# A new hand-written order of steps for a cross-attention kernel with a snake-activated feed-forward network

## The chip, the cores and the metric

The kernel runs on one core of one Trainium2 chip. Five engines work side by side: TensorE (PE in the profile, with its weight loads shown apart as PEld), VectorE (DVE), ScalarE (ACT), GpSimd (POOL) and SyncE (SP). Each engine takes its instructions strictly in the order in which the program gives them to it. The time is device microseconds for one launch, the median of several runs.

## The reference, cut to what matters

```python
B, H, S, Ns, D = (8, 8, 512, 32, 64)          # x: B,H,S,D    state: B,H,Ns,D
n_tokens, d_model, d_ff = (4608, 512, 2048)

def _attn_ref(x, state):
    scale = 1.0 / np.sqrt(D)
    a = softmax(scale * np.matmul(x, state.transpose(0, 1, 3, 2)))    # over the 32 states
    xread = np.matmul(a, state)
    a2 = softmax(scale * np.matmul(state, x.transpose(0, 1, 3, 2)))   # over the 512 positions
    sread = np.matmul(a2, x)
    return np.concatenate([xread, sread], axis=2)

def _moe_ref(x, w_in, w_out, alpha):
    h = x @ w_in
    s = np.sin(alpha * h)
    g = h + s * s / (alpha + 1e-09)
    return g @ w_out
```

(`softmax` stands here for the reference's four lines of maximum, exp, sum and division.) The result of the first function, as 8 batches of 512 + 32 tokens with 512 features each, is the input of the second. All inputs and the output are float32; the kernel computes in bfloat16 with float32 sums.

## The kernel before

**Tiles.** The 4352 tokens are cut into nine tiles: tile t = 0 to 7 holds the 512 positions of batch t, tile 8 the 8 x 32 state tokens of all batches. A tile is carried through 16 slices f of 128 hidden features. For tiles 0 to 7 the kernel does not multiply x-reads by `w_in`. It first forms M = state x `w_in` for the batch (steps `m`, `me`), and then h = M x softmax weights, two matmuls of 512 columns for each f. Tile 8 takes four matmuls of 256 columns with `w_in`.

**Steps.** The class `Steps` has one short method for each kind of step, and the string `ORDER` lists some 1,380 steps, each with its arguments, in the order in which they are emitted. That one list fixes the order of every engine's instructions, of every DMA queue, and of the eight PSUM banks (the bank number stands at the end of a PE step that opens a new result). The steps that matter here:

- `h.t.f.bank` (line 537; 543 for tile 8; `hg`, line 552, is one half of it): h of tile t, slice f, on PE. `si.t.f` (560): the sine on ACT. `sq.t.f.E` (201 on POOL or DVE, 569 on ACT): its square on engine E, where A is ACT, V is DVE and G is POOL. `gt.t.f` (576): g = s2 * (1/alpha) + h on DVE, which reads h from PSUM a last time and so sets its bank free.
- `o.t.st.f0.f1` (587): output rows st = 0 to 3 of the tile, slices f0 to f1, one PE matmul of 512 columns for each f; its weights are g. `oc.t.st.E` (595) copies the finished bank, `os` (602, 605) sends it to HBM from SP's queue. `oh`, `och`, `osh` are the same for 384 and 128 columns of one block of tile 7.
- For batch b: `lx` loads x (POOL's queue), `pk` (348) sorts it, `td` (389) transposes it by a DMA from SP's queue, `sc` (399) makes the scores on PE, `ex` (406) the exp on ACT, `rs`, `rr` (410, 416) sum and reciprocal on DVE, `nm` (201) the softmax weights on POOL, `ad` (440) their transpose by a DMA from SP's queue, after which `h.b` may start. Batch 1 transposes x on PE (`xt`, 376, copied by `xc`), batch 0 does both on PE (`xtq`, `at`). `w` (450), `cs` (461), `rc`, `xs` are the second softmax.
- `m.b.s.banks` (488) and `me.b.s.g.E` (496): slice s of M in two halves g, and their copies. `st_t`, `st_c` (340): the transposed states of batches 2 to 7; `s01_t`, `s01_k` (316) those of batches 0 and 1.
- `lq` loads x of batch 0 from SP's queue; `l_st`, `li.s`, `lo.s` load the states and the four slices of `w_in` and `w_out` from POOL's queue. `consts`, `zero` clear constant tiles on DVE, `exp_table` and `sin_table` (226) make ACT load a function table early, and `warm_up.n.cols.bank` (303) issues n matmuls on the cleared tile `warm`, whose result nobody reads.

**Buffers.** The two tiles that `si` and `sq` write come out of one ring of 10, the g tiles out of a ring of 38, the output tiles out of a ring of 6. The next of each waits until the oldest has been read.

```python
    for step in ORDER:
        name, *args = step.split(".")
        getattr(steps, name)(*(int(a) if a.isdigit() else a for a in args))
```

Of the kernel before, what the change touches and what calls it, by code (L numbers as in the profile page):

```python
# [21 lines left out]
touch_x l_s01 zero.1 touch lq.0.S ident_ consts warm_up.2.128.0 warm_up.2.128.1 warm_up.2.128.2  # L22
l_alpha lq.1.S zero.0 warm_up.6.512.3 exp_table lq.2.S identf.V lq.3.S s01_c.G l_st li.0 xq.0.A
s01_t.4 li.1 xtq.0.5 xq.1.A s01_k.1.V s01_k.0.A li.2 xtq.1.6 xc.0.0.0.V xq.2.A xc.0.0.1.V lo.0
al_t.7 xq.3.A xtq.2.0 al_c inva sc.0.0.1 lo.1 xc.0.1.0.A xtq.3.2 warm_up.2.128.3 ex.0.0
warm_up.2.128.4 lx.1.0.1 warm_up.2.128.5 xc.0.1.1.V warm_up.2.128.6 warm_up.2.128.7 rs.0.0 sc.0.1.0
li.3 st_t.0.3 ex.0.1 rr.0.0 st_t.1.4 lo.2 st_c.0.0.V st_c.0.1.A warm_up.2.128.5 warm_up.2.128.6
warm_up.2.128.1 st_c.1.0.A rs.0.1 warm_up.2.128.2 warm_up.2.128.7 nm.0.0.0.4.G warm_up.2.128.0
warm_up.2.128.5 st_c.1.1.A warm_up.2.128.3 warm_up.2.128.6 warm_up.2.128.1 rr.0.1 warm_up.2.128.2
sin_table warm_up.2.128.7 warm_up.2.128.0 nm.0.1.0.4.G at.0.0.5 warm_up.2.128.3 ac.0.0.V m.0.0.6.4  # L30
m.1.0.1.2 lo.3 at.0.1.7 me.0.0.0.V me.0.0.1.A warm_up.2.128.0 warm_up.2.128.3 me.1.0.1.A ac.0.1.V
hg.0.2.0.5 me.1.0.0.V hg.0.1.0.4 hg.0.2.1 hg.0.1.1 hg.0.0.0.0 lx.2.0.1 si.0.2 hg.0.0.1 m.1.1.6.3
si.0.1 m.0.1.7.2 hg.0.3.0.1 me.0.1.1.A sq.0.2.V hg.0.3.1 sq.0.1.G me.1.1.0.V me.1.1.1.A
# [12 lines left out]
si.0.12 o.0.0.10.11 o.0.3.9.11 sq.0.13.G ad.1 hg.0.15.0.2 sq.0.12.A o.0.1.10.12 hg.0.15.1 gt.0.12
o.0.2.8.10 si.0.15 o.0.2.10.11 gt.0.13 o.0.0.11.12 hg.0.14.0.4 sq.0.15.A hg.0.14.1 o.0.3.11.13
si.0.14 gt.0.15 o.0.0.12.13 o.0.1.12.13 o.0.3.13.14 sq.0.14.A pk.2.0.V o.0.1.13.14 pk.2.1.V h.1.2.5
gt.0.14 h.1.4.6 td.2 si.1.2 lx.3.0.1 h.1.0.2 si.1.4 o.0.0.13.15 sq.1.2.V h.1.1.4 si.1.0 gt.1.2
sq.1.4.G o.0.3.14.16 si.1.1 o.0.2.11.13 sq.1.0.A oc.0.3.V h.1.6.5 sq.1.1.G gt.1.4 o.0.2.13.14 os.0.3  # L50
h.1.3.0 si.1.6 gt.1.0 o.0.1.14.16 si.1.3 sq.1.6.G h.1.13.6 gt.1.1 oc.0.1.A o.0.2.14.15 o.0.0.15.16
si.1.13 h.1.15.2 sq.1.3.G gt.1.6 os.0.1 o.0.2.15.16 oc.0.0.A h.1.5.4 sq.1.13.G oc.0.2.V si.1.15
h.1.7.3 os.0.0 gt.1.3 o.1.1.0.1.5 si.1.5 os.0.2 h.1.8.1 sq.1.15.G gt.1.13 o.1.1.1.2 si.1.7
o.1.2.0.2.7 sq.1.5.A o.1.1.2.3 sq.1.7.G h.1.12.0 gt.1.15 si.1.8 h.1.9.6 gt.1.5 o.1.2.2.3 si.1.12
sq.1.8.G o.1.2.3.5 gt.1.7 si.1.9 o.1.1.3.4 h.1.10.2 sq.1.12.A pk.3.1.V h.1.11.4 sq.1.9.G gt.1.8
o.1.2.5.6 si.1.10 o.1.2.6.7 gt.1.12 h.1.14.3 si.1.11 sq.1.10.G o.1.2.7.8 gt.1.9 sc.2.1.1 si.1.14
o.1.1.4.7 sq.1.11.A pk.3.0.V sq.1.14.G o.1.1.7.8 gt.1.10 td.3 o.1.2.8.9 sc.2.0.0 o.1.1.8.9 gt.1.11
# [606 lines left out]
```

## Time and profile before

| what | value |
|---|---|
| median of 8 runs (lowest to highest) | 221.3 us (220.83 to 222.78) |
| the profiled execution: its own time / its span | 220.93 us / 219.0 us |
| PE busy, matmuls | 210.2 us (96%), 1593 recorded |
| ACT, DVE, POOL busy | 173.3 us (79%), 162.0 us (74%), 107.0 us (49%) |
| `o` matmuls (line 587) | 133.9 us busy, 542 recorded |
| `h` matmuls (line 537) | 60.0 us busy, 219 recorded |
| warm-up matmuls (line 303) | 7.4 us busy, 66 recorded |
| DMA transposes, issue to landing (median) | x 4.3 us (6 of them), softmax weights 3.2 us (7) |

The span runs from the first to the last instruction of the program, and the time of a run has about 2 us around it. A matmul's record is longer than the distance to the next one, since matmuls overlap; so the distance from start to start is what a matmul costs PE when it is kept fed. Some matmul records are missing (1593 of 1619), while every weight load is there; so the steps were found in the trace by their weight loads. Idle time is shown in brackets with what ended it.

### The profile page before, as it was taken

Reading aid. Unit: us, or ns where it says so; the run is one execution under the profiler, and the core shown is the slowest. Engines: PE = TensorE matmul, PEld = TensorE weight load, DVE = VectorE, ACT = ScalarE, POOL = GpSimd, SP = SyncE. Lnnn points to the kernel's source line nnn. Section 1 sums busy time; section 2 is a strip of 40 time slices with the busy share of each in tenths; the row PEclk is TensorE's granted clock in tenths of the full one; section 3 lists DMA queues with packets and bytes.
Section 4 is the critical chain, followed back from the end, with each engine's and each line's share of the span. In section 5 each row is a group of like instructions: output and inputs, shape, how many; then the busy total and the mean of one; then the engine's idle time right before and its main releaser. Section 6 shows DMA issues by size and latency. Waiting matters only on the chain.

```text
span 219.0 us, 4304 instructions
## 1 busy us (share of the span) xinstructions
PE 210.2 (96%) x1593; PEld 104.6 (48%) x1619; DVE 162.0 (74%) x286; ACT 173.3 (79%) x297; POOL 107.0 (49%) x115
## 2 busy tenths in 40 slices
PE   6889999999999999999999999999999999999994
PEld 2744544444444534444454444454445555665452
DVE  2769896999768889989888788888667987661201
ACT  4799878997899979898996999798848896785111
POOL 5968533895296657753943387273501082121000
PEclk9999999999999999999999999999999999999999
DMA  6999999945487529167145327480220211012042
GB/s 200 193 199 201 205 203 133 207 124 96 99 166 123 99 95 139 58 144 95 49 82 133 107 70 96 136 108 0 48 100 3 96 48 48 0 51 96 1 143 97
DMA packets 38052, 23.48 MB, mean 107 GB/s; under 512 B 20992, under 2 KB 33680, under 8 KB 38032
## 3 DMA queue, kind: packets, MB, share of 16 engines
q1 hardware_dynamic: 26128, 15.08, 27.2%
q0 software_dynamic: 11648, 8.13, 26.2%
q8 instruction: 12, 0.20, 0.4%
q14 instruction: 8, 0.07, 0.1%
q10 hardware_dynamic: 256, 0.01, 0.1%
HBM read 17.44 MB, written 8.91 MB: 120 GB/s over the span
## 4 chain that ended last, share of the span: by engine, by line
PE 88%; ACT 4%; DVE 4%; issue 2%; POOL 2%
PE o_ps L587 52%; PE h_ps L537 20%; PE m_ps L488 4%; PE h_ps L543 3%; PE h_ps L552 3%; DVE gT L576 2%; PE warm_ps L303 2%; PE w_ps L450 2%; POOL s L201 2%; PE s_ps L399 1%; PE w_ps L461 1%; ACT s L560 1%; ACT stT L340 1%; ACT L226 1%; ACT M L496 1%
## 5 line engine op out<-in xcount | busy, mean ns | idle before, releaser
L587 PE MATMUL o_ps<-w_out_sb,gT 128*128 128x512 bf16 (+2 forms) x542 | 133.9, 373 | 1.6 <-issue 1.0
L576 DVE SCALAR_TENSOR_TENSOR gT<-s,inva_sb,h_ps 128x512 bf16<-128x512 bf16 (+1 forms) x144 | 96.6, 714 | 19.1 <-POOL s L201 9.7
L201 POOL TENSOR_TENSOR s<-s 128x512 bf16<-128x512 bf16 (+1 forms) x76 | 76.6, 1019 | 63.8 <-ACT s L560 62.0
L560 ACT ACTIVATE s<-h_ps,alpha_sb 128x512 bf16<-128x512 f32 (+1 forms) x144 | 88.7, 670 | 10.6 <-PE h_ps L543 4.5
L587 PEld LDWEIGHTS <-gT 128*128 128x128 bf16 x560 | 52.4, 98 | 60.3 <-issue 5.0
L537 PE MATMUL h_ps<-AT,M 128*128 128x512 bf16 x219 | 60.0, 379 | 0.3
L537 PEld LDWEIGHTS <-M 128*128 128x128 bf16 x224 | 21.8, 98 | 25.9 <-issue 0.4
L569 ACT ACTIVATE s<-s 128x512 bf16<-128x512 bf16 (+1 forms) x53 | 31.4, 594 | 0.8
L201 POOL TENSOR_TENSOR A<-E,rR 128x512 bf16<-128x512 bf16 x16 | 16.6, 1056 | 23.6 <-ACT o_sb L595 12.7
L595 ACT COPY o_sb<-o_ps 128x512 f32<-128x512 f32 (+2 forms) x24 | 13.7, 571 | 16.6 <-PE o_ps L587 16.5
L496 ACT CAST M<-m_ps 128x512 bf16<-128x512 f32 x35 | 18.6, 594 | 8.2 <-PE m_ps L488 8.2
L496 DVE CAST M<-m_ps 128x512 bf16<-128x512 f32 x29 | 18.9, 679 | 2.7 <-PE m_ps L488 2.5
L595 DVE COPY o_sb<-o_ps 128x512 f32<-128x512 f32 x11 | 7.6, 690 | 13.0 <-PE o_ps L587 12.9
L410 DVE TENSOR_REDUCE R<-E 128x16 f32<-128x512 bf16 x16 | 10.4, 658 | 1.3 <-ACT E L406 1.1
L201 DVE TENSOR_TENSOR s<-s 128x512 bf16<-128x512 bf16 (+1 forms) x15 | 6.2, 414 | 6.4 <-ACT s L560 6.4
L488 PE MATMUL m_ps<-w_in_sb,stT 64*32 64x512 bf16 x256 | 10.2, 382 | 0.3 <-DMA w_in_sb<-in_moe_w_in_dram 0.3
L468 DVE RECIPROCAL rC<-w_ps 128x128 f32<-128x128 f32 x8 | 7.6, 948 | 3.3 <-PE w_ps L461 3.2
L303 PE MATMUL warm_ps<-warm 128*128 128x128 bf16 (+1 forms) x66 | 7.4, 265 | 2.2 <-DVE warm L209 2.0
L543 PE MATMUL h_ps<-xs_all,w_in_sb 128*128 128x256 bf16 x64 | 9.1, 273 | 0.0
L406 ACT ACTIVATE E<-s_ps 128x512 bf16<-128x512 f32 x16 | 8.9, 603 | 0.3 <-PE s_ps L399 0.2
L552 PE MATMUL h_ps<-AT,M 128*128 128x512 bf16 x29 | 8.4, 379 | 0.6 <-ACT M L496 0.5
L560 ACT ACT_TABLE_LOAD x5 | 6.4, 1283 | 2.2 <-PE h_ps L537 1.1
(56 smaller groups left out, 100.7 us busy)
## 6 DMA issues: line engine op xcount, KB each, us to landing
out_dram<-o_sb SPq DMA_DIRECT2D x33, 256.0 KB, 2.3
xnat<-in_x_dram POOLq DMA_DIRECT2D x7, 512.0 KB, 7.9
w_in_sb<-in_moe_w_in_dram POOLq DMA_DIRECT2D x4, 512.0 KB, 10.8
w_out_sb<-in_moe_w_out_dram POOLq DMA_DIRECT2D x4, 512.0 KB, 17.9
x<-in_x_dram SPq DMA_DIRECT2D x4, 256.0 KB, 3.9
st_nat<-in_state_dram POOLq DMA_DIRECT2D x1, 256.0 KB, 4.6
out_dram<-o_sb SPq DMA_DIRECT2D x1, 192.0 KB, 1.9
s<-in_state_dram SPq DMA_DIRECT2D x1, 128.0 KB, 2.2
```

Of the source, the lines that this page charges most:

```text
L201: {"V": k.nc.vector, "G": k.nc.gpsimd}[eng].tensor_tensor(out, a, b, ALU.mult)
L303: k.nc.tensor.matmul(wp[:, :cols], k.warm[:, 0:k.P], k.warm[:, :cols], start=True, stop=True)
L488: k.nc.tensor.matmul(k.t["m", b, s + n, g][o0:o0 + k.Ns, :], k.stT[k.half(r), b * k.G + g, c0:c0 + k.Ns], k.w_in_sb[k.half(r), 2 * g + h, ...
L496: k.copy(eng)(k.t["M", b][:, g, s * k.FW:(s + 1) * k.FW], k.t["m", b, s, g][:])
L537: k.nc.tensor.matmul(hp[:, :n], k.t["M", t][:, g, fs], k.t["AT", t][:, g, :], start=(g == 0), stop=(g == k.G - 1),)
L543: k.nc.tensor.matmul(hp[:, :n], k.w_in_sb[:, q, fs], k.xs_all[:, q].rearrange("p b j -> p (b j)"), start=(q == 0), stop=(q == k.Q - 1),)
L552: k.nc.tensor.matmul(k.t["h", t, f][:], k.t["M", t][:, g, f * k.P:(f + 1) * k.P], k.t["AT", t][:, g, :], start=(g == 0), stop=(g == k.G - 1),)
L560: k.nc.scalar.activation(s[:, :n], k.t["h", t, f][:, :n], ACT.Sin, scale=k.alpha_sb[:, f:f + 1])
L569: k.nc.scalar.activation(s2[:, :n], s[:, :n], ACT.Square)
L576: k.nc.vector.scalar_tensor_tensor(gT[:, :n], k.t["s2", t, f][:, :n], k.inva_sb[:, f:f + 1], k.t["h", t, f][:, :n], ALU.mult, ALU.add,)
L587: k.nc.tensor.matmul(k.t["o", t, st, half][:, cols], k.t["gT", t, f][:, rows], k.w_out_sb[:, f, cols], start=(f == 0), stop=(f == k.FT - 1),)
L595: k.copy(eng)(o_sb[:, cols], k.t["o", t, st, half][:, cols])
```

## The change

Only `ORDER` differs. The same loads, copies, matmuls and transfers are made, with the same tiles; nearly every step stands in another place and many banks differ. 1,380 steps become 1,374. What the new list does:

- `consts` comes ahead of both `zero` steps (before, `zero.1` was first on DVE). The warm-up ahead of the first input is 7 matmuls of 512 columns in place of 6 of 128 and 6 of 512. Of the other warm-ups, three groups of 3, 5 and 3 now stand between the first transposes of x, and some behind `at` and `m.0.1` are gone: 59 of 128 columns where there were 60.
- `st_t.1` and its copies come ahead of `st_t.0`, and `sin_table` stands behind one of the four copies and not behind all.
- `td` and `ad` keep their rank among the steps of their batch, but the steps that wait for them stand elsewhere.
- Engines of some steps change: `oc` on ACT 22 to 18 and on DVE 11 to 15; `me` on ACT 35 to 33 and on DVE 29 to 31; `sq` on ACT 53 to 56, on POOL 76 to 75, on DVE 15 to 13; `st_c` on ACT 3 to 2, on DVE 1 to 2.
- At the end, the last six slices of `o.7.1` are kept until after `o.8` and are mixed with `o.7.2`; `oh.7.3.0` stands earlier.

The parts of the diff that are spoken of below:

```diff
-touch_x l_s01 zero.1 touch lq.0.S ident_ consts warm_up.2.128.0 warm_up.2.128.1 warm_up.2.128.2
-l_alpha lq.1.S zero.0 warm_up.6.512.3 exp_table lq.2.S identf.V lq.3.S s01_c.G l_st li.0 xq.0.A
...
-li.3 st_t.0.3 ex.0.1 rr.0.0 st_t.1.4 lo.2 st_c.0.0.V st_c.0.1.A warm_up.2.128.5 warm_up.2.128.6
-warm_up.2.128.1 st_c.1.0.A rs.0.1 warm_up.2.128.2 warm_up.2.128.7 nm.0.0.0.4.G warm_up.2.128.0
-warm_up.2.128.5 st_c.1.1.A warm_up.2.128.3 warm_up.2.128.6 warm_up.2.128.1 rr.0.1 warm_up.2.128.2
-sin_table warm_up.2.128.7 warm_up.2.128.0 nm.0.1.0.4.G at.0.0.5 warm_up.2.128.3 ac.0.0.V m.0.0.6.4
...
-si.0.14 gt.0.15 o.0.0.12.13 o.0.1.12.13 o.0.3.13.14 sq.0.14.A pk.2.0.V o.0.1.13.14 pk.2.1.V h.1.2.5
-gt.0.14 h.1.4.6 td.2 si.1.2 lx.3.0.1 h.1.0.2 si.1.4 o.0.0.13.15 sq.1.2.V h.1.1.4 si.1.0 gt.1.2
-sq.1.4.G o.0.3.14.16 si.1.1 o.0.2.11.13 sq.1.0.A oc.0.3.V h.1.6.5 sq.1.1.G gt.1.4 o.0.2.13.14 os.0.3
-h.1.3.0 si.1.6 gt.1.0 o.0.1.14.16 si.1.3 sq.1.6.G h.1.13.6 gt.1.1 oc.0.1.A o.0.2.14.15 o.0.0.15.16
-si.1.13 h.1.15.2 sq.1.3.G gt.1.6 os.0.1 o.0.2.15.16 oc.0.0.A h.1.5.4 sq.1.13.G oc.0.2.V si.1.15
-h.1.7.3 os.0.0 gt.1.3 o.1.1.0.1.5 si.1.5 os.0.2 h.1.8.1 sq.1.15.G gt.1.13 o.1.1.1.2 si.1.7
...
-o.7.0.8.9 oc.8.1.A o.7.0.9.10 oc.8.0.V o.7.0.10.12 os.8.1 o.7.0.12.13 os.8.0 o.7.0.13.16 o.7.2.0.2.2
-oc.7.0.A o.7.2.2.5 os.7.0 o.7.2.5.11 oh.7.3.0.1 o.7.2.11.13 och.7.3.0.A o.7.2.13.15 osh.7.3.0
-o.7.2.15.16 oh.7.3.1.4 oc.7.2.V os.7.2 och.7.3.1.A osh.7.3.1
+touch_x l_s01 consts touch lq.0.S ident_ l_alpha lq.1.S zero.0 warm_up.7.512.3 exp_table lq.2.S
+zero.1 identf.V lq.3.S s01_c.G l_st li.0 xq.0.A xtq.0.4 warm_up.3.128.3 li.1 xq.1.A s01_t.5
+xc.0.0.0.V li.2 xtq.1.6 warm_up.5.128.3 xq.2.A s01_k.1.V lo.0 al_t.7 s01_k.0.A xc.0.0.1.V xtq.2.0
+warm_up.3.128.3 xq.3.A al_c sc.0.0.1 inva lo.1 xc.0.1.0.A xtq.3.2 warm_up.2.128.3 warm_up.2.128.4
+lx.1.0.1 ex.0.0 warm_up.2.128.5 xc.0.1.1.V warm_up.2.128.6 warm_up.2.128.7 sc.0.1.0 rs.0.0 st_t.1.3
+li.3 ex.0.1 st_t.0.4 rr.0.0 lo.2 st_c.1.1.A st_c.1.0.V warm_up.2.128.5 warm_up.2.128.6 sin_table
+warm_up.2.128.2 rs.0.1 warm_up.2.128.7 warm_up.2.128.1 nm.0.0.0.4.G warm_up.2.128.0 warm_up.2.128.5
+warm_up.2.128.3 warm_up.2.128.6 warm_up.2.128.2 rr.0.1 warm_up.2.128.7 warm_up.2.128.1 st_c.0.1.V
+warm_up.2.128.0 warm_up.2.128.5 nm.0.1.0.4.G st_c.0.0.A at.0.0.3 warm_up.2.128.6 ac.0.0.V m.0.0.2.7
+m.1.0.1.0 lo.3 at.0.1.5 me.0.0.1.V me.0.0.0.A warm_up.2.128.6 me.1.0.1.A ac.0.1.V hg.0.2.0.4
+hg.0.0.0.3 me.1.0.0.V hg.0.2.1 hg.0.1.0.2 hg.0.0.1 si.0.2 lx.2.0.1 hg.0.3.0.6 hg.0.3.1 si.0.0
+m.0.1.7.5 hg.0.1.1 me.0.1.1.A warm_up.2.128.0 sq.0.2.V warm_up.2.128.1 sq.0.0.G me.0.1.0.V si.0.1
+m.1.1.0.1 warm_up.2.128.5 gt.0.2 me.1.1.1.A hg.0.5.0.7 sq.0.1.G hg.0.6.0.5 hg.0.5.1 si.0.3 gt.0.0
+hg.0.6.1 m.0.2.1.4 si.0.5 me.1.1.0.V sq.0.3.G hg.0.4.0.3 me.0.2.0.A hg.0.4.1 me.0.2.1.V hg.0.7.0.0
+si.0.4 hg.0.7.1 sq.0.5.G hg.0.10.0.1 gt.0.1 hg.0.10.1 si.0.6 hg.0.9.0.4 hg.0.9.1 gt.0.3 sq.0.4.G
...
+o.0.0.14.16 oc.0.3.A h.1.2.1 oc.0.0.V h.1.0.5 lx.3.0.1 si.1.2 o.0.2.14.16 si.1.0 os.0.0 h.1.1.4
+sq.1.2.V os.0.3 h.1.3.0 oc.0.2.V si.1.1 sq.1.0.G h.1.4.2 gt.1.2 si.1.3 os.0.2 o.0.1.13.15 sq.1.1.G
+o.0.1.15.16 gt.1.0 si.1.4 h.1.15.6 h.1.8.7 sq.1.3.A oc.0.1.V sq.1.4.G o.1.1.0.1.1 si.1.15
+o.1.2.0.1.5 gt.1.3 os.0.1 h.1.6.3 si.1.8 gt.1.1 sq.1.15.G h.1.12.0 si.1.6 gt.1.4 h.1.7.4 si.1.12
+sq.1.8.G o.1.1.1.3 sq.1.6.A gt.1.15 h.1.5.2 sq.1.12.G o.1.2.1.2 gt.1.8 si.1.7 h.1.13.6 si.1.5
+o.1.1.3.4 gt.1.6 h.1.11.7 sq.1.7.G si.1.13 o.1.1.4.5 gt.1.12 h.1.9.3 sq.1.5.A o.1.2.2.3 sq.1.13.G
+gt.1.7 h.1.10.0 si.1.11 o.1.2.3.4 gt.1.5 o.1.2.4.5 si.1.9 h.1.14.4 sq.1.11.G gt.1.13 sc.2.0.2
...
+o.8.0.8.10 oc.8.1.V o.8.0.10.13 os.8.1 o.8.0.13.16 o.7.2.0.2.1 oc.8.0.V o.7.2.2.5 os.8.0 o.7.2.5.13
+o.7.1.10.11 o.7.2.13.15 o.7.1.11.13 o.7.2.15.16 o.7.1.13.15 oc.7.2.A o.7.1.15.16 oh.7.3.1.3 os.7.2
+oc.7.1.A os.7.1 och.7.3.1.A osh.7.3.1
```

## The prediction

> **What bounds the kernel now.** I read four views. First the page's busy row and the table of stretches, to see who is never idle; then the waits of PE; then the timeline of the tightest stretch; last the start.
>
> ```profile
> PE 210.2 (96%) x1593; PEld 104.6 (48%) x1619; DVE 162.0 (74%) x286; ACT 173.3 (79%) x297; POOL 107.0 (49%) x115
> ...
> 0.00:10.00 10.00, 7.27 (x98) 4.90 (x99) 4.71 (x15) 5.77 (x10) 7.70 (x16) 1.00 0.86 196
> 10.00:20.00 10.00, 8.86 (x117) 4.99 (x117) 7.62 (x15) 9.60 (x18) 7.58 (x9) 1.00 1.22 201
> 20.00:30.00 10.00, 9.84 (x93) 5.13 (x93) 9.31 (x17) 8.66 (x14) 4.68 (x5) 1.00 1.30 204
> 40.00:50.00 10.00, 9.95 (x54) 4.65 (x54) 9.72 (x17) 9.96 (x18) 9.52 (x10) 1.00 0.57 146
> 120.00:130.00 10.00, 9.84 (x80) 4.74 (x80) 7.44 (x15) 9.14 (x15) 5.47 (x6) 1.00 0.38 112
> ```
>
> (Columns: stretch, its length, busy time of PE, PEld, DVE, ACT, POOL, clock, DMA share, GB/s.) PE is busy from about 17 us on; only the first 17 us and the last 3 have air. In 40 to 50 us ACT, DVE and POOL are full as well: there the new order has nothing to spare.
>
> ```profile
> PE warm_ps L303 <- DVE warm L209: 2.0, 1, 2.0
> PE o_ps L587 <- issue: 1.0, 6, 0.2
> PE x_ps L361 <- ACT xp L356: 0.7, 1, 0.7
> PE h_ps L552 <- ACT M L496: 0.5, 1, 0.5
> PE m_ps L488 <- DMA w_in_sb<-in_moe_w_in_dram: 0.3, 1, 0.3
> ...
> PEld L399 <- DMA xT<-xp: 0.2, 1, 0.2
> ```
>
> These are PE's waits of the whole run, and the one weight load that waited for a transpose. No wait for a softmax-weight transpose is there. Three lines of the start and four of the stretch from 37 us, with the prices used below:
>
> ```profile
> 2.61 2.76 PE L303 MATMUL warm_ps<-warm 128*128 128x512 bf16 x6
> 11.59 1.28 ACT L226 ACT_TABLE_LOAD   x1
> 12.10 0.63 PE L488 MATMUL m_ps<-w_in_sb,stT 64*32 64x512 bf16 x16 [0.28 <-DMA w_in_sb<-in_moe_w_in_dram]
> ...
> 37.49 2.42 ACT L560 ACTIVATE s<-h_ps,alpha_sb 128x512 bf16<-128x512 f32 x4 [0.43 <-PE h_ps L537]
> 40.20 2.84 DVE L576 SCALAR_TENSOR_TENSOR gT<-s,inva_sb,h_ps 128x512 bf16<-128x512 bf16 x4
> 41.22 9.67 POOL L201 TENSOR_TENSOR s<-s 128x512 bf16<-128x512 bf16 x9 [0.19 <-ACT s L560]
> 50.65 2.54 PE L587 MATMUL o_ps<-w_out_sb,gT 128*128 128x512 bf16 x11
> ```
>
> Start to start, an `o` or `h` matmul costs PE (2.54 - 0.38)/10 = 0.216 us, a sine ACT (2.42 - 0.70)/3 = 0.57, a g DVE (2.84 - 0.75)/3 = 0.70, a square POOL 9.67/9 = 1.07. I call PE's time at these distances its slots (16 `m` matmuls 0.56, a `w` step 0.47, a `cs` step 0.29, eight `sc` matmuls 0.24). From `m.0.2` on, the old list holds 196.1 us of slots; the trace takes from 17.25 to 215.96, 198.7 us. The 2.6 us between them sit at some thirty changes of matmul shape (`m`, `cs`, `sc`), 0.1 to 0.2 each. So behind 31 us the old order has no dependency wait on PE that can be seen, and a new order can win almost nothing there; it can only lose.
>
> **The change part by part.**
>
> *Memsets and warm-up, ahead of 8 us.* `zero.1` (0.70 us on DVE) leaves the front, so PE starts at 1.3 and not 2.0. Seven matmuls at 0.427 end near 4.3 (before: 5.3), so `xtq.0` starts behind its cast (4.90) near 5.0 instead of 5.64. But the end of this chain is ACT: it waits for `lq.2` (landed 6.06), then has `xq.2`, one copy, `xq.3`, `xc.0.1.0`, and `ex.0.0` starts near 8.1 as before. Behind that, `nm.0.0` waits for POOL, which issues DMAs until 10.1 in both lists, and `m.0.0` for `li.0` (landed 12.05). The loads keep their order on SP and POOL; the DMA share is 0.86 to 1.30 until 40 us, so landings stay. Value 0; without that cover, up to -0.6. `zero.1` itself is only needed at 9.6: 0.
>
> *The clock.* The six 512-column warm-ups ran at 0.427 us, half rate, and the transposes of x from 5.64 on at 0.056 (full rate), after 3.3 us of unbroken PE work. The Trainium skill, "TensorE: Matmul & The Clock Gate", section "What's actually happening", says that the full clock is granted after about 3.4 us of sustained work in a window that runs freely. This speaks against the change: its first burst is 3.0 us and then PE waits 0.6 us for the cast. By the trace's row the cost is 0; by the rule some 30 matmuls of 128 columns would cost 0.107 instead of 0.056 until the next window, 1.5 us of slower PE work, most of it inside waits for ACT. Behind it lies the wait for `li.0`. I take 0 and keep 0.3 as the end.
>
> *Table load and state copies, 9 to 13 us.* `sin_table` (1.28 + 0.2 us) moves ahead of one ACT copy, so ACT is free at 12.4 and not 13.1 when `m.0.0` is done. Against it: the copies into stT ran one after the other across ACT and DVE (10.12 waited for DVE's), so `rs.0.1` on DVE goes 0.5 later, `nm.0.1` 0.3 later; `at.0.1` stands behind `m` on PE (12.65) anyway. First sine 0.1 earlier.
>
> *Tile 0 until 28 us.* When `li.2` lands (17.21) PE will have done four `hg` more than before: 4 x 0.216 = 0.86 us ahead. Then `hg.0.7.0` needs the bank that `me.1.1.0.V` frees; I get 18.4 from DVE's queue (`gt.0.2`, `gt.0.0` behind POOL's square at 17.0, then the copy); `hg.0.10.0` needs `me.0.2.0.A`, 18.8, behind two sines. `m.1.2` (0.28) now comes later, `o.0.3.7` waits 0.2 for `gt.0.7`. `xt.1` cannot start before `lx.1` (25.10). Walking on, `m.0.3` starts at 28.05 against 28.02, with 185.4 us of slots left against 185.6. Sum -0.2; ends -0.9 (all kept) and +0.5.
>
> *Transposes.* Room in PE slots between emission and first user: `ad.1` 3.45 to 4.60, `ad.2` 3.06 to 4.46, `td.4` 4.96 to 5.74, `td.7` 7.9 to 12.3; less for `ad.4` (13.1 to 9.4) and `ad.6` (6.5 to 5.6). In the trace `ad.1` lands at 36.46 and `h.1.2` starts at 36.59, with PE fed: nothing is waited for, nothing is won. Only runs in which transposes land later can win: at most about 0.4, the distance of the median to the profiled run.
>
> *Tile 1, the place that decides.* The room behind `ad.1` is made by doing tile 0's `o` work before `h.1.2`. Before, 12 `o` slots of tile 0 (2.6 us) stood between the first h of tile 1; now 5 (1.1 us). From h to its first `o`, f 0 had 5.6 us and now has 3.24; h to g took 3.2 us at best and 3.7 in the median for POOL squares of this tile. On top, three `oc` copies (3 x 0.69) now stand on DVE between the first g, where two did. I walked the queues with the prices above, 0 at the start of `h.1.2`: POOL has ten squares without a break from 2.0 to 12.6; `gt.1.3` ends at 5.1, `gt.1.1` at 5.7, `gt.1.8` at 8.0, `gt.1.5` at 10.8. `h.1.12` wants `h.1.3`'s bank at 4.96, `h.1.7` wants `h.1.1`'s at 5.4, `h.1.11` wants `h.1.8`'s at 7.6, `sc.2.0` wants `h.1.5`'s at 10.1. With each wait pushing the rest, PE loses about 0.2 four times: +0.8 (0 to +1.5).
>
> *Tiles 2 to 8.* The same walk gives tile 2 0.15 (`h.2.10`, `o.2.0.12`), tile 3 0.1 (`h.3.11`). For tiles 4 to 8 I find no wait above 0.1. Allow +0.35 in all (0 to +1.2). SP: each `td`, `ad` holds up the `os` behind it, and six output tiles cover that. POOL: `lx.2` stands ahead of `sq.0.0` in both. Engine moves: DVE gains about 3 us of work, ACT loses 2, of 219; beside PE, except in tile 1.
>
> *Tail.* `os.7.2`, `os.7.1` and `osh.7.3.1` leave within 1.2 us of each other. Before, `os.7.2` was issued at 215.82, landed at 217.85, and `osh.7.3.1` (64 KB) landed 0.27 later; at that rate 256 KB more is 1.1 us, of which most is moved before PE ends. +0.2 (-0.1 to +0.6).
>
> Sum: 0 - 0.2 + 0.8 + 0.35 + 0.2 = +1.15, less a little for late transposes in other runs: about +1.0. Against the profiled execution that is 220.93 + 1.0 = 221.9; its median stands 0.37 higher, so 222.3.
>
> **The rivals.** *The queues keep up (not slower).* If the squares of tile 1 find ACT and POOL free earlier than I walked, `gt.1.3` ends before 4.9 and no bank is late; then the head start of 0.2 to 0.9 stays. For it: the old tile 1 was as full (9.52 to 9.96 of 10 us) and PE waited for nothing. Against: it had 1.5 us more `o` work in between. 221.3 - 0.2 + 0.2 = 221.3; with the whole 0.9 kept, 220.4.
>
> *A second jam (clearly slower).* g rings, sine ring and banks are as tight in other places: `sq.3.13.A` waits for `gt.3.2`, `h.6.3` and `h.7.10` for banks. If waits of 0.2 come in six or more places behind tile 2, or the clock stays low past 12 us (32 `m` and 12 `hg` at half rate, about +1.5), it is +2.0 to +2.7: 223.3 to 224.0.
>
> *The transposes are no matter.* This is my own case for the profiled run; then the new room earns 0 and only its price is seen.
>
> **How the numbers follow.** Tile 1 and small waits: 0.55, between 221.5 and 223.0, half of it on either side of 222.4. Queues keep up: 0.27, two thirds within 0.5%, one third below 220.2. A second jam: 0.18. A change of 0.5%, 1.1 us, is about what a measurement of this kernel can tell from none. Faster by more: 0.10; within: 0.44; slower by more: 0.46. The range 220.4 to 223.9 goes from the head start kept whole to most of the second jam.
>
> **What would show it.** Right: PE's waits list lines 537 and 399 behind DVE's gT between 39 and 52 us, 0.5 to 1 us in all; `m.0.2` at 17.25 and `m.0.3` near 28.0; waits for transposes stay near 0; the table load starts near 10.0. Wrong: `m.0.3` before 27.5, no PE wait in tile 1, matmuls at 0.427 after 5.3 us, or more than 1.5 us of waits behind 60 us.

## The result, and the profile after

The changed kernel takes 224.52 us in the median of 11 runs (223.54 to 225.71); the kernel before, in 32 runs beside it, 221.29 us. The ratio of their times is 1.0137, with a 95% interval from 1.0114 to 1.0161: about 3.2 us slower, three times the 1.0 us that the forecast had, and outside its range. The profiled execution took 225.38 us (span 223.5), so it is one of the slower ones; this matters below.

The table of stretches of the changed kernel, in the same columns as before (stretch, its length, busy time of PE, PEld, DVE, ACT, POOL, clock, DMA share, GB/s):

```profile
0.00:10.00 10.00, 7.80 (x55) 4.91 (x56) 3.42 (x12) 5.34 (x9) 7.71 (x16) 1.00 0.84 184
10.00:20.00 10.00, 9.62 (x148) 6.17 (x148) 8.17 (x17) 7.86 (x15) 6.19 (x8) 1.00 1.24 206
20.00:30.00 10.00, 9.54 (x86) 4.55 (x86) 8.73 (x16) 8.76 (x16) 5.80 (x6) 1.00 1.30 204
40.00:50.00 10.00, 9.66 (x45) 4.36 (x45) 9.52 (x15) 9.81 (x18) 7.59 (x8) 1.00 1.10 207
120.00:130.00 10.00, 9.79 (x124) 4.55 (x126) 9.70 (x20) 7.31 (x13) 2.83 (x3) 1.00 0.57 133
```

In the first 10 us PE is busy longer than before (7.80 for 7.27 us) with barely half the instructions (55 for 98): it works slowly there. From 40 to 50 us it lost 0.3 us of busy time. The busy share over the whole span is 96%, as before, and tells nothing.

The waits of PE, and one line of the waits of DVE, first after and then before (total, times, longest):

```profile
PE h_ps L536 <- DVE gT L575: 1.2, 3, 0.6
PE warm_ps L302 <- DVE warm L208: 1.2, 1, 1.2
PE x_ps L360 <- ACT xp L355: 1.0, 1, 1.0
PE o_ps L586 <- issue: 0.8, 5, 0.2
PE o_ps L586 <- DVE gT L575: 0.4, 1, 0.4
```

```profile
DVE xp L347 <- DMA xnat<-in_x_dram: 3.3, 3, 2.2
DVE xp L348 <- DMA xnat<-in_x_dram: 1.0, 2, 0.8
```

(The lines of the changed kernel are one lower than before.) PE now waits 1.6 us for `gT`, which it never did before: 0.27 of it in tile 1, the rest behind three loads of x. The DVE line, which the prediction did not use, says that DVE waits for these loads. The timeline of the changed kernel around the three (start, duration, engine, line; in brackets the idle time ahead and what ended it):

```profile
64.96 0.94 POOL L274 DMA_DIRECT2D xnat<-in_x_dram  x1
65.05 1.24 SPq L439 DMA_TRANSPOSE AT<-A  x1
...
72.51 1.20 DVE L347 COPY xp<-xnat 128x1024 bf16<-128x1024 bf16 x1 [0.20 <-DMA xnat<-in_x_dram]
...
75.61 0.59 PE L536 MATMUL h_ps<-AT,M 128*128 128x512 bf16 x2 [0.59 <-DVE gT L575]
...
90.17 0.94 POOL L274 DMA_DIRECT2D xnat<-in_x_dram  x1
90.26 1.24 SPq L439 DMA_TRANSPOSE AT<-A  x1
...
98.30 0.43 DVE L347 COPY xp<-xnat 128x1024 bf16<-128x1024 bf16 x1 [0.90 <-DMA xnat<-in_x_dram]
...
99.44 1.45 PE L536 MATMUL h_ps<-AT,M 128*128 128x512 bf16 x6 [0.34 <-DVE gT L575]
...
109.44 0.94 POOL L274 DMA_DIRECT2D xnat<-in_x_dram  x1
...
118.50 0.76 DVE L347 COPY xp<-xnat 128x1024 bf16<-128x1024 bf16 x2 [2.21 <-DMA xnat<-in_x_dram]
...
119.98 1.46 PE L586 MATMUL o_ps<-w_out_sb,gT 128*128 128x512 bf16 x6 [0.44 <-DVE gT L575]
```

Read the second as a chain. `lx.5` is issued at 90.17 and lands 8.1 us later; `pk.5` has stood at the head of DVE's queue since 97.4. DVE works in order, so the `gt` steps behind `pk.5` are late too, and at 99.44 PE waits for one of them. `lx.6`, issued at 109.44, takes 9.0 us; DVE stands still for 2.21 us. `lx.4`, at 64.96, is late by 0.20 us only; the rest of that delay is the packing itself, one copy of which takes 1.20 us where others take 0.42. The three such places (`pk.4`, `pk.5`, `pk.6`) cost PE 0.75, 0.50 and 0.60 us, found as the jumps of PE's actual starts against the sum of its slots. The matmuls that wait are the first of `h.2.15`, `h.3.11` and `o.4.3`. The weights of a matmul are loaded ahead of it (those of `h.3.11` at 98.73, while its first matmul starts at 99.44), so a wait is easily put one step too late: some of the expectations below call the first two places `o.2.3` and `h.3.10`.

The start of the changed kernel:

```profile
1.19 3.17 PE L302 MATMUL warm_ps<-warm 128*128 128x512 bf16 x7 [1.19 <-DVE warm L208]
...
5.36 0.61 PE L360 MATMUL x_ps<-ident,xp 128*128 128x128 bf16 x4 [1.00 <-ACT xp L355]
...
14.00 0.62 PE L487 MATMUL m_ps<-w_in_sb,stT 64*32 64x512 bf16 x16
```

The first transposes of the kernel before, eight in the time of four:

```profile
5.65 0.62 PE L361 MATMUL x_ps<-ident,xp 128*128 128x128 bf16 x8
```

In this execution PE's clock record turns to full speed at 10.5 us; before, it did so at 5.2. Until then transposes follow each other at 0.107 us instead of 0.056, and `m.0.3` starts at 30.34 us instead of 28.02, with 0.2 us less of slots left behind it. So against the profiled execution of before the trace splits its 4.45 us into 2.1 at the start and 2.35 behind `m.0.3`, of which 1.85 are the three places above. The medians show a smaller total, 3.2. Whether the start of the typical run is late as well was the first thing to test.

### The profile page after: what moved, and what is told of

Same layout as the page of the kernel before. It is cut to its first block, busy times and chain, and to the rows that moved or that the text cites. A ratio compares the mean times of both kernels' runs of the same rounds, so it can differ in the third digit from the quotient of the medians.

```text
span 223.5 us, 4291 instructions
## 1 busy us (share of the span) xinstructions
PE 214.0 (96%) x1593; PEld 106.0 (47%) x1619; DVE 165.8 (74%) x291; ACT 173.1 (77%) x293; POOL 103.6 (46%) x114
## 4 chain that ended last, share of the span: by engine, by line
PE 66%; DMA 9%; ACT 7%; issue 6%; DVE 5%; POOL 5%; SPq 0%; POOLq 0%
PE o_ps L586 40%; PE h_ps L536 12%; DMA xnat<-in_x_dram 8%; POOL s L200 4%; DVE gT L575 3%; PE h_ps L542 3%; ACT s L559 3%; PE m_ps L487 2%; PE h_ps L551 2%; DMA x<-in_x_dram 2%; PE s_ps L398 1%; PE w_ps L449 1%; ACT M L495 1%; PE w_ps L460 1%; PE x_ps L360 1%
## 5 line engine op out<-in xcount | busy, mean ns | idle before, releaser
L200 POOL TENSOR_TENSOR s<-s 128x512 bf16<-128x512 bf16 (+1 forms) x75 | 73.4, 995 | 59.1 <-ACT s L559 57.7
L536 PE MATMUL h_ps<-AT,M 128*128 128x512 bf16 x218 | 60.6, 379 | 1.4 <-DVE gT L575 1.2
L568 ACT ACTIVATE s<-s 128x512 bf16<-128x512 bf16 (+1 forms) x56 | 34.1, 612 | 1.1
L495 DVE CAST M<-m_ps 128x512 bf16<-128x512 f32 x31 | 20.0, 679 | 8.1 <-PE m_ps L487 7.9
L495 ACT CAST M<-m_ps 128x512 bf16<-128x512 f32 x33 | 18.0, 590 | 9.4 <-PE m_ps L487 9.2
L594 ACT COPY o_sb<-o_ps 128x512 f32<-128x512 f32 (+2 forms) x20 | 11.4, 570 | 15.9 <-PE o_ps L586 15.6
L594 DVE COPY o_sb<-o_ps 128x512 f32<-128x512 f32 x15 | 10.3, 688 | 6.2 <-PE o_ps L586 6.1
L409 DVE TENSOR_REDUCE R<-E 128x16 f32<-128x512 bf16 x16 | 10.5, 662 | 1.6 <-ACT E L405 1.6
L302 PE MATMUL warm_ps<-warm 128*128 128x128 bf16 (+1 forms) x66 | 9.1, 290 | 1.2 <-DVE warm L208 1.2
L551 PE MATMUL h_ps<-AT,M 128*128 128x512 bf16 x31 | 8.9, 380 | 0.2
L347 DVE COPY xp<-xnat 128x1024 bf16<-128x1024 bf16 x14 | 6.5, 490 | 3.3 <-DMA xnat<-in_x_dram 3.3
L542 PEld LDWEIGHTS <-w_in_sb 128*128 128x128 bf16 x64 | 6.3, 98 | 3.1
```

The source lines that it names most:

```text
L200: {"V": k.nc.vector, "G": k.nc.gpsimd}[eng].tensor_tensor(out, a, b, ALU.mult)
L409: k.nc.vector.reduce_sum(R[:, g], k.t["E", b][:, g].rearrange("p c (h j) -> p (c h) j", j=k.Ns), axis=AX.X)
L495: k.copy(eng)(k.t["M", b][:, g, s * k.FW:(s + 1) * k.FW], k.t["m", b, s, g][:])
L536: k.nc.tensor.matmul(hp[:, :n], k.t["M", t][:, g, fs], k.t["AT", t][:, g, :], start=(g == 0), stop=(g == k.G - 1),)
L542: k.nc.tensor.matmul(hp[:, :n], k.w_in_sb[:, q, fs], k.xs_all[:, q].rearrange("p b j -> p (b j)"), start=(q == 0), stop=(q == k.Q - 1),)
L551: k.nc.tensor.matmul(k.t["h", t, f][:], k.t["M", t][:, g, f * k.P:(f + 1) * k.P], k.t["AT", t][:, g, :], start=(g == 0), stop=(g == k.G - 1),)
```

## The experiments

Theory C: the clock comes on late, and the start carries the loss. Theory L: late loads of x hold DVE, and with it `gT` and PE. Every run is compared with the kernel before on the same chip in the same session; its median was 221.2 to 221.5 us throughout.

**A longer opening burst.**

```diff
-zero.0 warm_up.7.512.3 exp_table
+zero.0 warm_up.10.512.3 exp_table
```

> The changed kernel with one step altered: the opening burst has 10 matmuls of 512 columns instead of 7, so that TensorE is busy from 1.2 to about 5.4 us, up to the first transposes of x.
> - Theory C (the clock: the shorter burst and the idle stretch behind it leave TensorE at half speed until 10.5 us, and the slow steps of the start push everything behind them): the clock is granted by 5.5 us, the first slice of M (m.0.0) starts at 12.1 to 12.4 instead of 13.99, the last slice for tile 0 (m.0.3) at 28.1 to 28.7 instead of 30.34, and the time falls by 1.4 to 2.1, to 222.4 to 223.1 us. The waits of VectorE for the x loads stay.
> - Rival (the start is late because of the new order of its steps and loads, whatever the clock): within 0.4 us of 224.5.
> - Theory L (late loads of x) alone: within 0.4 us of 224.5.

Measured: 225.66 us, ratio 1.0148 (1.0101 to 1.0195). In its profile the clock came on at 5.3 us, `m.0.3` started at 28.31, and that one execution took 223.66, 1.7 us less than the profiled one of the changed kernel, as Theory C says. But it is the fastest of six, and their median did not fall; a gain of some tenths stays possible within the interval. One profile had confirmed the theory where the runs did not.

**The three loads earlier.**

```diff
 nm.2.1.0.4.G
+lx.4.0.1
...
 sc.4.1.6
+lx.5.0.1
...
 m.4.0.1.4.3.5
+lx.6.0.1
```

(each taken out where it stood)

> The changed kernel with three steps moved in the written order and nothing else: lx.4, lx.5 and lx.6 (the loads of x of batches 4 to 6) are issued earlier by some 10, 9 and 4 us of TensorE work.
> - Theory L (in the changed order these loads stand too close ahead of their packing on VectorE, which stops in order and holds back gT): VectorE's waits for the loads (3.3 us) fall below 0.5, the waits of o.2.3, h.3.10 and o.4.3 behind them (1.85 us) go, and the time falls by 1.3 to 1.9, to 222.6 to 223.2 us. The start is as late as it was (m.0.3 at 30.3).
> - Rival (these waits only stand where another wait would: the banks or the ScalarE chain are as late): the waits for loads go, the time falls by less than 0.5.
> - Rival 2 (the earlier loads collide with the transposes or the outputs): new waits on ad or os, time as before or up by to 1 us.

Measured: 228.70 us, ratio 1.0313 (1.0261 to 1.0364); the second rival came true, and worse. The waits for the loads were gone, but this stood in the waits of PE, and in the timeline:

```profile
PE h_ps L536 <- DMA AT<-A: 3.6, 1, 3.6
```

```profile
57.18 0.94 POOL L274 DMA_DIRECT2D xnat<-in_x_dram  x1
57.26 2.42 SPq L439 DMA_TRANSPOSE AT<-A  x1
...
65.87 2.33 PE L536 MATMUL h_ps<-AT,M 128*128 128x512 bf16 x10 [3.61 <-DMA AT<-A]
```

`lx.4` now leaves in the same moment as `ad.2`. Both take about 8.5 us, where `ad.2` had taken 3.9 and `lx.4` 7.5, and tile 2 cannot start. Part of the loss is the clock: the profiled execution, at 226.41 us, had a mean granted clock of 1.0, but the other five, at 227.66 to 229.95, had 0.985 to 0.992. This is the case in which the room behind a transpose does matter.

**Both.**

> Both edits at once: the opening burst of 10 matmuls and the three loads of x issued earlier.
> - Theories C and L together: the gains add, 220.8 to 221.8 us; what is left over the kernel before is the wait in tile 1 (0.4 us).
> - If either edit moves a wait and does not remove it, the sum falls short: 222.4 or more.

Measured: 227.26 us, ratio 1.0207 (1.0149 to 1.0265). The same wait for `ad.2` (2.8 us), so nothing could add; here the profile shows the clock fall to half behind the wait (last section).

**Fewer spare matmuls.** Of the spare matmuls between `nm.0.0` and `nm.0.1`, twelve are left out.

```diff
-warm_up.2.128.3 warm_up.2.128.6 warm_up.2.128.2 rr.0.1 warm_up.2.128.7 warm_up.2.128.1 st_c.0.1.V
-warm_up.2.128.0 warm_up.2.128.5 nm.0.1.0.4.G
+warm_up.2.128.3 rr.0.1 st_c.0.1.V nm.0.1.0.4.G
```

> The changed kernel without 12 of the 128-column spare matmul pairs' 24 instructions ahead of the first transpose of the softmax weights: six of nine pairs behind nm.0.0 are left out (no result uses them). The cold clock stays as it is.
> - Theory C, first form (spare matmuls in front of at.0.0 are on TensorE's path once the start is late): at.0.0 starts at 12.7 instead of 13.52, and the time falls by 0.3 to 0.9, to 223.6 to 224.2.
> - Theory C, second form (what is late is the chain of ScalarE and VectorE steps behind the slow transposes and scores, and at.0.0 only waits beside it): at.0.0 earlier, but the first hg and m.0.3 where they were, and the time within 0.3 us of 224.5.

Measured: 225.31 us, ratio 1.0144 (1.0095 to 1.0193): no gain. In its profile the clock was on by the first transposes, with the same opening as the changed kernel (`m.0.3` at 28.23, time 223.53). So when the clock comes on differs from execution to execution, with nothing changed ahead of it.

**The start by itself.** Three kernels are cut off behind the stores of tile 0.

> The kernel before, cut off behind the outputs of tile 0: the written order up to the last store of tile 0, without the h, sin, square, gT, output matmuls, copies and stores of tile 1 and without the later batches' packing; what it leaves out is all outputs but tile 0's. It measures the start and tile 0 by themselves, and how far they vary from run to run.
> - Theory C (the start decides, and the moment at which the clock comes on varies from run to run): some 40 to 46 us, in two groups 1.5 us apart, as the kernel before as a whole (221.2 and 222.8).
> - Rival D (the spread comes from waits behind tile 1): all runs within 0.5 us.

> The changed kernel cut off in the same way (the same work left out, only tile 0's outputs written).
> - Theory C: slower than the cut kernel before by 1 to 2 us in the median, and spread over about 2 us; so the start holds 1 to 2 of the 3.2 us.
> - Rival D (the loss of the timed runs lies behind tile 0, and the late clock of the one profile is an exception): within 0.5 us of the cut kernel before, spread below 0.5.

> The changed kernel cut off in the same way, with the opening burst of 10 matmuls instead of 7.
> - Theory C: 0.5 to 1.8 us faster than the cut changed kernel, and most runs in its lowest group: the burst reaches the first transposes.
> - Rival C2 (the clock may come on late however long the burst is, by the moment in which its window falls): as spread as the cut changed kernel, and the same median within 0.5.
> - Rival D: the same as the cut changed kernel, without spread.

Measured: cut before 48.77 us (47.78 to 49.61, in two groups 1.5 us apart), cut changed kernel 48.50 (47.60 to 49.22), cut with the long burst 47.67 (46.86 to 48.28). In the cut kernel before, PE waits 0.9 us near the end only because tile 1's work is missing there; with that taken off, the changed start is some 0.6 us slower in the median of six (1.05 if the lower three runs of each are compared), not 2. The profile had shown a late clock that also meets the kernel before. Most of the loss of the typical run had to lie behind tile 0.

**lx.5 and lx.6 alone earlier**, so that no load leaves with `ad.2`.

> The changed kernel with lx.5 and lx.6 alone issued earlier (lx.5 behind sc.4.1, lx.6 behind the first slice pair of batch 4's M); lx.4 stays where it was, so that no load of x lies on the queues beside the second transpose of softmax weights.
> - Theory L (late loads hold VectorE): the two waits of pk.5 and pk.6 go and o.4.3 and h.3.10 no longer wait (1.1 us of TensorE in the profile): 0.9 to 1.3 us faster than the changed kernel, which at a median of 224.5 to 225.4 makes 223.3 to 224.4. The transpose of batch 2's weights is not delayed.
> - Rival (the loads collide wherever they are put): a wait for AT or for xT of another batch appears, and nothing is gained.

Measured: 222.56 us (9 runs), ratio 1.0050 (1.0020 to 1.0080). Two moved steps bring back 2.0 of the 3.2 us. The waits of DVE, and the timeline at the two packings:

```profile
DVE xp L347 <- DMA xnat<-in_x_dram: 0.4, 1, 0.4
```

```profile
96.75 0.72 DVE L347 COPY xp<-xnat 128x1024 bf16<-128x1024 bf16 x1
...
103.75 0.94 POOL L274 DMA_DIRECT2D xnat<-in_x_dram  x1
...
115.15 0.85 DVE L347 COPY xp<-xnat 128x1024 bf16<-128x1024 bf16 x2
```

No bracket stands behind the packings: nothing is waited for. `lx.6` took 5.8 us instead of 9.0, `ad.4` 3.1 instead of 7.3, and the waits at `h.3.11` and `o.4.3` are gone. That is 1.1 us in the profile. The medians of the times say 2.0 and those of the spans 1.6 (222.25 to 220.70), so either the loads are later still in the other runs, or the rest lies elsewhere.

**The converse in the kernel before.** Its `lx.5` is issued behind `sq.3.0.G`, its `lx.6` behind `sq.4.1.G`.

> The converse in the kernel before: lx.5 is issued later (behind the square sq.3.0 on GpSimd, so at 85.3 instead of 81.4 us) and lx.6 later (behind sq.4.1, at 105.4 instead of 98.8); nothing else changes. They then stand 7.3 and 5.4 us ahead of their packing instead of 11.2 and 12, about as in the changed kernel (7.2 and 6.9).
> - Theory L: VectorE waits for both loads (in the profile 1 us or more each), TensorE waits behind gT, and the time rises by 1.0 to 2.0, to 222.3 to 223.3 us.
> - Rival (the room between load and packing decides only in the changed order, whose h and output matmuls follow each other more closely): waits of VectorE, but under 0.4 us on the time.

Measured: 221.60 us, ratio 1.0022 (0.9996 to 1.0048). The rival was nearer. Here `lx.5` landed in 5.9 us instead of 7.7 and `lx.6` in 6.2, so DVE did not wait for either. The room between load and packing is therefore not the cause by itself: these two loads land in time when they leave alone. In the kernel before, `lx.5` leaves with `ad.4` as well, and both are slow (7.7 and 6.9 us), but its packing comes 11.2 us later:

```profile
81.35 0.94 POOL L275 DMA_DIRECT2D xnat<-in_x_dram  x1
81.43 1.24 SPq L440 DMA_TRANSPOSE AT<-A  x1
...
92.58 0.75 DVE L348 COPY xp<-xnat 128x1024 bf16<-128x1024 bf16 x2
```

**The kernel before with the opening alone changed, long burst.**

> The kernel before with the opening alone changed: the warm-up tile cleared first and 10 matmuls of 512 columns from 1.2 us, instead of 6 of 128 and 6 of 512 columns from 2.0; the state's clearing moved behind.
> - Theory C2 (the start is equal in both orders in the median, and a burst without a gap up to the first transposes saves the runs in which the clock comes on late): the slow group of the kernel before (222.7) goes or shrinks; median 220.2 to 221.0, so 0.3 to 1.0 faster.
> - Rival (li.0, which lands at 12.05 us in the kernel before, sets the start whatever the clock): the low group stays at 221.1 to 221.3, median within 0.3 of the kernel before.

Measured: 221.24 us, ratio 0.9987 (0.9963 to 1.0011). The lower group did not move, and the upper group was not met: 12 runs lie between 220.89 and 221.46, while 4 of the 35 runs of the kernel before beside them lie at 222.66 and above. With so few, twelve runs do not show that the burst does away with them.

**Loads and burst; and lx.4 one step earlier** (ahead of `nm.3.1` instead of behind it).

> The changed kernel with lx.5 and lx.6 earlier and the burst of 10 matmuls.
> - If the two causes add (loads 2.0, burst 0.8 as in the cut kernels): 221.6 to 222.0 us.
> - Rival (the burst gains nothing in the whole kernel, as its one full run seemed to say): 222.3 to 222.8.

> As the last, and lx.4 issued one step earlier on GpSimd (ahead of the second normalization of batch 3 instead of behind it), so 1 us earlier and still after the transpose of batch 2's weights has landed.
> - Theory L: VectorE's wait for lx.4 (0.2 to 0.4 us) goes, but the packing's own 1.6 us on VectorE stays in front of gT: 0.1 to 0.4 faster than the last, 221.3 to 221.8.
> - If the wait at o.2.3 (0.75 us in the profile) hangs on the load alone: 0.6 to 0.8 faster, 220.9 to 221.2.

Measured: 222.93 us, ratio 1.0064 (1.0041 to 1.0088), and 222.44 us, 1.0041 (1.0016 to 1.0065). The burst gains nothing on top of the loads in the median of the times; the spans fell by 0.2 us (220.70 to 220.50), but the time outside the span was about 2.5 us in 10 of the 12 runs, for 2 of 9 without the burst. Issuing `lx.4` earlier takes away its DVE wait and the 0.75 us at `h.2.15` in the profile. It now leaves two microseconds ahead of `ad.3` and still takes 7.7 us: it is in time because it left earlier, not because it left alone, and the copy of `pk.4` takes 0.42 us instead of 1.20, for a reason that was not looked into. The medians show 0.5, between the two expectations, with intervals that overlap.

**The transpose moved, not the load.**

```diff
-lx.5.0.1 ad.4 h.3.8.0
+lx.5.0.1 h.3.8.0
...
-os.2.2 o.2.1.9.10
+os.2.2 ad.4 o.2.1.9.10
```

> The changed kernel with one step moved: the transpose ad.4 is issued behind the store os.2.2 (at about 93 us instead of 90.26). The loads of x stay where the changed order has them.
> - Theory M (the meeting: a load of x is late where a transpose leaves with it): lx.5 lands within 6.5 us of its issue instead of 8.1, pk.5 no longer waits (0.9 us in the profile), h.3.10 does not wait behind gT (0.5 us), and the time falls by 0.4 to 1.0; ad.4 lands before h.4.8 needs it at 100.
> - Theory L (the room alone): pk.5 still waits 0.5 us or more for lx.5 and the time stays within 0.3.
> - Third way: ad.4 lands behind 100 us, h.4.8 waits for it, and the time rises by up to 2.

Measured: 224.10 us, ratio 1.0104 (1.0054 to 1.0153). The timeline:

```profile
88.67 0.94 POOL L274 DMA_DIRECT2D xnat<-in_x_dram  x1
91.66 1.51 SPq L439 DMA_TRANSPOSE AT<-A  x1
...
95.81 0.73 DVE L347 COPY xp<-xnat 128x1024 bf16<-128x1024 bf16 x1
...
116.67 0.76 DVE L347 COPY xp<-xnat 128x1024 bf16<-128x1024 bf16 x2 [2.38 <-DMA xnat<-in_x_dram]
```

With the transpose 3 us behind it, `lx.5` lands in 5.9 us, in the same place of the order; `pk.5` does not wait (no bracket at 95.81), nor does `h.3.11`. `ad.4` itself still takes 5.8 us. `lx.6`, which was not touched, is as late as ever (2.38 us). For `lx.5` in this place the meeting with the transpose is thus shown to be the cause: one trace here and one of the converse (5.9 us each) stand against six with the meeting, in both orders (7.6 to 8.3). The gain in time, 0.4 us, is of the expected size but within the intervals.

**lx.5 alone earlier.**

> The changed kernel with lx.5 alone issued earlier (76 us), away from ad.4; lx.6 and lx.4 where the changed order has them.
> - Theory M: lx.5 lands in 6 to 7 us and ad.4 in 2 to 3 instead of 7.3; 0.5 to 1.0 faster than the changed kernel, and the wait for lx.6 (2.2 us of VectorE, 0.6 to 0.7 of TensorE at o.4.3) stays, so 0.6 to 1.2 slower than the run with both loads moved (222.6).
> - Rival (lx.6 follows lx.5 in its queue and lands in time once lx.5 is gone): as fast as the run with both.

Measured: 224.22 us, ratio 1.0113 (1.0063 to 1.0163). `lx.5` took 7.8 us, more than expected, but in time; `ad.4` took 3.1, `pk.5` did not wait, `pk.6` still waited 1.9 us and `o.4.3` behind it 0.6. So of the 2.0 us that both loads bring, `lx.6` has the larger part by the medians, some 1.6, though the intervals overlap.

**Another end of the order; a copy of tile 1 on ACT**, both on top of the last kernel with all three loads earlier and the long burst (222.44 us).

> The corrected changed kernel (burst of 10, lx.4, lx.5 and lx.6 earlier; 222.44 us) with another end of the written order: the last output matmuls of o.7.1, its copy and its store come ahead of those of o.7.2, so that two of the three last stores no longer leave within 0.7 us. The sum of TensorE's work is the same.
> - Theory E (the stores that end together cost about half a microsecond behind the last instruction in half of the runs): 0.3 to 0.6 faster, 221.9 to 222.1, and the time outside the span 1.9 us in nearly all runs.
> - Rival (that half microsecond has another source): within 0.2 of 222.44, and the time outside the span still 2.4 to 2.6 in half of the runs.

> As the last, and in tile 1 the output copy oc.0.1 on ScalarE instead of VectorE (0.7 us out of the chain of gT just ahead of the banks that h.1.12 and h.1.7 wait for).
> - If the jam of tile 1 is VectorE's: the waits of h.1.7 and o.1.1 (0.45 us) go: 0.3 to 0.5 faster than the last.
> - If ScalarE is as tight there: the sines come 0.6 us later, the waits stay or grow: within 0.3 of the last, on either side.

Measured: 222.67 us, ratio 1.0040 (1.0015 to 1.0065), and 222.85 us, 1.0049 (1.0023 to 1.0074). Neither gains. The time outside the span is now 2.3 to 2.6 us in all 24 runs of the two, so the stores that end together are not what makes it long. In tile 1 the wait at `h.1.12` went and that at `h.1.7` fell from 0.23 to 0.11 us, but `h.1.6` now waits 0.34 us for the copy on ACT and `h.1.11` 0.35: more in all than before.

**The two openings exchanged.** The kernel before with the changed opening (7 matmuls from 1.2 us); the changed kernel with `lx.5`, `lx.6` earlier and the old opening.

> The kernel before with the changed kernel's opening and nothing else of it: the warm-up tile cleared first, 7 matmuls of 512 columns from 1.2 us, no 128-column ones ahead, the state's clearing behind.
> - Theory C (the gap of 1.2 us or more between this burst and the first transposes makes a late clock frequent): the slow group (222.7 and up), a sixth to a third of the runs of the kernel before, becomes half or more of the runs, and the median rises to 221.8 to 222.8.
> - Rival (the opening is no matter; the clock comes on late by chance in both): the two groups keep their shares, median within 0.3 of the kernel before.

> The changed kernel with lx.5 and lx.6 earlier (222.56 us with its own opening) and the opening of the kernel before: 6 matmuls of 128 and 6 of 512 columns from 2.0 us.
> - Theory C: the late starts become rarer: 0.5 to 1.0 faster, 221.6 to 222.1.
> - Rival: within 0.3 of 222.56.

Measured: 221.93 us, ratio 1.0012 (0.9988 to 1.0035), and 223.07 us, ratio 1.0072 (1.0050 to 1.0093). In the old order the new opening moves the median up by 0.8 us, with 9 of 12 runs between 221.79 and 222.28, where none of the 23 runs of the kernel before beside them lies (20 are at 221.59 or below); the interval of the ratio still includes no change. In the changed order the old opening gains nothing. The opening of the first:

```profile
1.19 3.17 PE L303 MATMUL warm_ps<-warm 128*128 128x512 bf16 x7 [1.19 <-DVE warm L209]
4.29 0.64 PE L309 MATMUL st_ps<-ident,s01b 128*64 128x128 bf16 x8
4.86 0.61 PE L361 MATMUL x_ps<-ident,xp 128*128 128x128 bf16 x4
6.23 0.61 PE L361 MATMUL x_ps<-ident,xp 128*128 128x128 bf16 x4 [0.76 <-ACT xp L356]
```

Four transposes take 0.61 us here, half speed. PE had been busy from 1.19 to 5.47 without a gap, and yet the clock came on only at 9.9 us. My gap behind the burst cannot be the reason in this execution.

## Why the prediction was wrong

**Tiles 2 to 8: the term that failed.** It stood at +0.35 (0 to 1.2), with 0.1 at `h.3.11` and "for tiles 4 to 8 I find no wait above 0.1". Measured in the trace: 1.85 us of waits at `h.2.15`, `h.3.11` and `o.4.3`; in time, 2.0 us for `lx.5` and `lx.6` and about 0.5 for `lx.4`. The walk priced PE slots, squares, sines, g and banks, and for the transposes their room; it took no account of the loads of x. Of a load I asked only which step it stood ahead of on POOL, not when it lands and who is next in line on DVE for it. For two of the loads the order itself has the answer: from `lx.5` to its packing there were 10.3 us of PE slots and now 7.7, from `lx.6` 8.5 and now 6.8, while the slowest load in the trace of before took 8.0 us behind 60 us. The table of DMA issues gave a median of 7.9. Both were there to be read. For `lx.4` the room did not shrink (7.1 and now 7.6); DVE waited longer for it before, 0.78 us, and PE did not wait at all. There the new order has `gt.2.6` close behind the packing, and `h.2.15` needs the bank that it sets free. Why `lx.6` takes 9.0 us, though it leaves with no transpose, stays open. So the second jam, the rival that had 0.18, is what came, by waits that it did not name, and the time went beyond its 224.0.

**The clock: sized by one row.** The term was 0, end 0.3. The changed kernel's profiled execution paid 2.1 us for it, more than the +1.5 of the second rival's "the clock stays low past 12 us". In the runs the term is smaller: the cut kernels put it at some 0.6, and the new opening in the old order gives +0.8 with an interval that includes 0. (That rival's +1.5 does not come out of the prediction's own prices either: 32 `m` and 12 `hg` at half rate are 3.7 us more.) Neither the row (clock on in the first 5.3 us) nor the rule of the Trainium skill, "TensorE: Matmul & The Clock Gate", section "What's actually happening", about 3.4 us of sustained work in a free-running window, can be read as a fixed time: the traces of this case show the clock on 2.7 us after the start of the work (cut kernel with the long burst), less than the page's figure, and not on after 4.3 us of it (the opening just shown). That the window runs freely would account for a spread; no run here shows the window itself. The prediction should have carried a spread here, not a value.

**Tile 0, apart from the clock: right.** With the clock on early, `m.0.2` and `m.0.3` of the new order started at 17.12 and 28.23 us (the kernel with less filling), against 17.25 before and 28.05 foretold. (The DMA share that the prediction gives as 0.86 to 1.30 until 40 us was 1.36 from 30 to 40; nothing hangs on it.)

**Transposes: right for the profile.** PE waits for none, before or after, and the room earned nothing that a run shows. Its price and its use were both seen: `ad.2` lands 0.7 us ahead of its user, and a load put beside it cost PE 3.6 us.

**Tile 1: right mechanism, half the size.** +0.8 was foretold, four waits of 0.2. The trace shows the first two of the four, 0.22 at `h.1.12` and 0.23 at `h.1.7`, in every profile of the new order that keeps the copy `oc.0.1` on DVE (the bracket below says 0.27, since the record of one matmul ahead is missing):

```profile
44.14 0.68 DVE L594 COPY o_sb<-o_ps 128x512 f32<-128x512 f32 x1
...
44.80 3.44 DVE L575 SCALAR_TENSOR_TENSOR gT<-s,inva_sb,h_ps 128x512 bf16<-128x512 bf16 x5
...
45.60 1.25 PE L536 MATMUL h_ps<-AT,M 128*128 128x512 bf16 x4 [0.27 <-DVE gT L575]
```

`h.1.12` starts when the first of these five g, `gt.1.3`, is done, as foretold; `h.1.11` and `sc.2.0` did not wait. That DVE's extra copy is the cause is not shown: with the copy on ACT these two waits shrank, but `h.1.6` ahead of them waited for the copy, so they came later anyway.

**Tail: right in size, by luck.** +0.2 was foretold, for stores that land later. From PE's end to the end of the span it took 3.1 us for 3.0. But in 4 of the 12 executions of the changed kernel on record the time outside the span is 2.4 to 2.5 us, against 1.8 to 2.0 in the others and in those of the kernel before: 0.2 on the mean. The stores that end together were tried as its cause and are not.

**The sum.** Two loads bring back 2.0 of the 3.2 us and the third some 0.5 (medians, in part of different sessions). But the best mended order, with all three and the long burst, stays at 222.44 us, 1.27 above the 221.17 of the kernel before beside it (ratio 1.0041), so that together they bring back about 2, not 2.5. The spans and times on record divide that rest: the median span is 220.05 us for 219.3, 0.75 more, of which the trace has 0.45 in tile 1; the time outside the span is 2.4 us for 1.9, the other 0.5. Where the last 0.3 us of the span come from, and what makes the time outside it, is not settled. No version was faster than the kernel before by more than the measurement tells.

## What to carry to other kernels

When a hand-written order is compressed or stretched, list every pair of issue and first use, loads included, and hold the room of each against the slowest landing of its kind in the trace, not the median; then ask which in-order engine stands still while it waits. Look at what leaves a queue in the same microsecond: where a load and a transpose started together here, the load was about a third slower and the transpose more than twice as slow, and moving either one took the wait for the load away. And take no cause from a single profile where runs vary: cutting the kernel off behind the suspect stage gave the median of that stage in one session.

## What the runs showed of the hardware

The transposes of softmax weights show the meeting most plainly: `ad.4` took 3.1 us where `lx.5` left well away from it, 5.8 where `lx.5` left 3.0 us ahead, 6.9 and 7.3 us where they left within 0.1 us of each other, and `ad.2` 8.6 us beside `lx.4`. Behind 55 us, loads of x (512 KB) that left within 0.1 us of a transpose took 7.4 to 8.8 us. Apart from one, most took 5.6 to 6.8 us, but `lx.5` took 7.2 to 8.2 in four kernels and `lx.4`, 2 us ahead of a transpose, up to 7.7, so the meeting is not all that delays a load. `lx.6` took 8.8 to 9.2 us in the five profiles in which it left 0.4 us ahead of a store, and 5.6 to 6.2 in the twelve others, where the next store left 1.5 us later or more; that the store is to blame was not tried by itself.

The moment at which the clock comes on is not fixed by the order. In profiles of kernels with the changed kernel's opening, seven matmuls up to about 4.4 us, it was recorded at 4.2, 4.7, 5.7, 9.2, 9.8 and 10.5 us, and at 9.9 with this opening in the old order. In all eight profiles with ten matmuls it came on between 3.8 and 6.5 us, so a burst that reaches the first transposes seems to help the clock, though of the medians only that of the cut kernel fell with it (by 0.8 us). And it can go again: behind the 2.8 us wait of the run with both edits it fell to half from 64.1 to 67.5 us, and the `h` matmuls of tile 2 followed each other at 0.43 us; behind the 3.6 us wait of the profile before, it did not.

The time outside the span is 1.9 us in the kernels of the old order and, in those of the new one, either 1.9 or about 2.45 us, in all 24 runs of two of them. It is in no trace, and its cause stays open.
